# Issuing the transfers of the row maxima from ScalarE's queue, one unit behind their split, in an adaLN block with sliding-window attention

## The chip, the cores and the metric

The kernel runs on one core of one Trainium2 chip. The metric is the time on the device in microseconds (us): the median of three runs, 703.54 us before the change (703.54, 703.71 and 696.3). One further execution was profiled; it took 700.14 us, of which 698.3 us lie between its first and its last instruction.

## The reference

A transformer block on x of 2048 rows by 448 columns, in float32, with six modulation vectors from a condition c. What matters here is the attention: 16 heads of 28 columns, each row sees itself and the 255 rows before it.

```python
mod = (_silu(c) @ w_mod).reshape(c.shape[0], 6, 1, -1)
h = _layernorm(x, axis=-1) * (1 + ca) + sa
scores = jnp.einsum("bhqd,bhkd->bhqk", q, k) * (Dh ** -0.5)
mask = (idx[:, None] - idx[None, :] >= 0) & (idx[:, None] - idx[None, :] < W)
p = _softmax(jnp.where(mask[None, None], scores, -1e9), axis=-1)
x = x + ga * ((p @ v) @ wo)
h = _layernorm(x, axis=-1) * (1 + cb) + sb
x = x + gb * (mish(h @ w1 + b1) @ w2)
```

## The kernel before, in words

The 2048 rows are worked on in four groups of 512. A matrix product is made in three passes over a high and a low part of each operand, so most results are split once by ScalarE (high part) and once by VectorE (low part).

**Three stages.** Up to about 60 us weights are loaded, the first layer norm and the first products for q, k and v are made. From about 60 to 395 us runs the attention, with the products of the next group, the output product of the last one and the loads of the second half's weights filled in between. After that come the two products of the second half (lines 807 and 989 to 991), where TensorE is busy without a break.

**Slots, units and quartets.** In the attention a *slot* is one head of one group, 64 in all. Four slots make a *quartet*. q and k go to DRAM (`scr`) and come back by `L` (line 562) with the 28 columns of a head in three copies, as 84 partitions. There are eight tiles for q (four pairs, `Q2`) and eight for k, so slot i takes the tiles of slot i-8.

- `A(i, t)` (lines 571 to 582) makes the scores of 128 rows (PE, tile `sA`, two banks) and VectorE takes each row's maximum under the mask (`mx`).
- `M2(pr)` (line 584) serves a *pair* of slots, 32 pairs in all: PE transposes the eight columns of maxima (`mt`), VectorE splits them into a high and a low part (`mr`, lines 588 and 589), and two transfers write these as partitions 84 and 85 of the pair's q tile, where k holds -1. So the next product gives score minus maximum.
- `B(u)` (line 604) is one of 192 *units*: PE writes the mask and then q times k into one of two banks `sB` (lines 620 and 622), ScalarE takes the exponential (`P`, line 625). Twelve units make a quartet: unit u belongs to slot 4*(u//12) + u%4.
- `PV` and `EV` (lines 627 and 639) multiply four units' `P` with v five units later, and ScalarE copies a quartet's result out (`o`).

**What sets the order.** Each engine and each queue works in the order of the program; the loop over units (lines 925 to 971) writes it out by hand. With r = u mod 12, the maxima of the next quartet's four slots are worked on by `A` in units 1 to 10; `M2` stands in r = 7 for its first pair and in r = 11 for its second (line 943). The four slots of the quartet after are loaded in r = 8, 11, 2 and 4 (line 945). The first pair's tile is read from the next quartet's unit 0 on, the second pair's from its unit 2 on. So the second pair has three units between `M2` and its first reader.

All transfers go through SyncE's queue (`dma`, line 58, so their line in the profile is 59). An instruction at its head that waits keeps all behind it waiting. The two transfers of `M2` wait for the split; the next slots' loads stand right behind them, and wait only until PE has read the tiles that they overwrite. Transfers share eight semaphores: one is issued only when the transfer that had its semaphore before, mostly eight places back in the program, has landed.

Of the kernel before, what the change touches and what calls it, by code (L numbers as in the profile page):

```python
# [8 lines left out]
F32 = mybir.dt.float32  # L9
# [11 lines left out]
NQ, NK, NV = 8, 8, 10  # L21
# [30 lines left out]
def adaln_block(ctx: ExitStack, tc: tile.TileContext, x, wqkv, wo, w1, b1, w2, c, w_mod, out):  # L52
    nc = tc.nc
    PE, ACT, DVE, POOL = nc.tensor, nc.scalar, nc.vector, nc.gpsimd
# [3 lines left out]
    def dma(o, i):  # L58
        nc.sync.dma_start(o, i)  # L59
# [25 lines left out]
    def bank(tag, bufs, name):  # L85
        return PS[0].tile([128, 512], F32, name=name, tag=tag, bufs=bufs)
# [14 lines left out]
    for k in range(4):  # L101
        t = st0.tile([112, 2 * D], F32, name=f"wm01_{k}")
# [10 lines left out]
    for part in range(3):  # L113
        for ci in range(4):
            r0, r1 = ci * 128, min(ci * 128 + 128, D)
            for h in ((slice(0, 128),) if ci < 3 else (slice(0, 64), slice(64, 128))):
                t = wqs[ci][h]
# [172 lines left out]
    def drain(*gs):  # L290
        for g in gs:
            for _ in g:
                pipe.step()
# [16 lines left out]
    def flush():  # L310
        while later:
            later.pop(0)()
# [117 lines left out]
    Q2 = [att.tile([86, 2, GT], F32R, name=f"q2_{i}") for i in range(NQ // 2)]  # L430
    Q3 = [Q2[i // 2][:, i % 2] for i in range(NQ)]
    K3 = []
    for i in range(NK):
        t = att.tile([86, GT + W], F32R, name=f"k3_{i}")
# [121 lines left out]


    NS = NG * H
    mx, Pt, pvb, et, O4 = {}, {}, {}, {}, {}
    junk = att.tile([128, 384], BF16, name="junk")  # L560

    def L(i):
        g, h = divmod(i, H)
        q, k = Q3[i % NQ], K3[i % NK]
        f0, f1 = h * DH, D + h * DH
        q0, k0 = g * GT, max(g * GT - W, 0)
        l0 = k0 - (g * GT - W)
        dma(q[0:84, :].bitcast(F32), scr[f0:f0 + DH, :, q0:q0 + GT].rearrange("d a n -> (d a) n"))
        dma(k[0:84, l0:].bitcast(F32), scr[f1:f1 + DH, :, k0:q0 + GT].rearrange("d a n -> (d a) n"))

    def A(i, t):
        g, h = divmod(i, H)
        q, k = Q3[i % NQ], K3[i % NK]
        if i % 2 == 0 and t == 0:
            mx[i // 2] = att.tile([128, 2, 4], F32, name=f"mx{i}", tag="mx", bufs=2)
        c0 = max(256 - 128 * t, 0) if g == 0 else 0
        p = bank("sA", 2, f"sA{i}_{t}")
        PE.matmul(p[:, c0:384], q[0:84, t * 128:(t + 1) * 128], k[0:84, t * 128 + c0:t * 128 + 384],  # L578
                  start=True, stop=True)
        DVE.tensor_tensor_reduce(out=junk[:, c0:384], in0=p[:, c0:384], in1=mask[:, c0:384], scale=1.0,  # L580
                                 scalar=-3.0e38, op0=ALU.add, op1=ALU.max,
                                 accum_out=mx[i // 2][:, i % 2, t:t + 1])

    def M2(pr):
        p = bank("tr", 1, f"mt{pr}")
        PE.transpose(p[0:8, 0:128], mx[pr].rearrange("p a t -> p (a t)"), ident)
        r = att.tile([8, 2, 128], F32R, name=f"mr{pr}", tag="mr", bufs=2)
        DVE.tensor_copy(r[:, 0], p[0:8, 0:128])
        DVE.tensor_tensor(r[:, 1], p[0:8, 0:128], r[:, 0].bitcast(F32), op=ALU.subtract)
        for i in range(2):  # L590
            dma(Q2[pr % (NQ // 2)][84 + i:85 + i].bitcast(F32).rearrange("o a (t n) -> o (a t) n", t=4),
                r[:, i].bitcast(F32))

    def units(g, b):
        return [x for x in BLOCKS[b] if g > 0 or x[0] >= 2]
# [8 lines left out]
    def B(u):  # L604
        i, b = unit(u)
        g, h = divmod(i, H)
        q, k = Q3[i % NQ], K3[i % NK]
        bl = units(g, b)
        c0 = bl[0][3]
        p = bank("sB", 2, f"sB{u}")  # L610
        far = {c + 128 * (jj - t0) for jj, t0, t1, c in bl if t0 <= jj < t1}
        diag = {c + 128 * (jj - 2 - t0) for jj, t0, t1, c in bl if t0 <= jj - 2 < t1}
        masked = []
        for c in sorted(far | diag):
            if c in far:
                masked.append((256 if c + 128 in diag else 128, c, 0))
            elif c - 128 not in far:
                masked.append((128, c, 128))
        for i, (n, c, m) in enumerate(sorted(masked)):
            PE.matmul(p[:, c:c + n], identr, fdmask[:, m:m + n], start=(i == 0), stop=False, skip_group_check=True)  # L620
        for jj, t0, t1, c in by_width(bl)[::-1]:
            PE.matmul(p[:, c:c + 128 * (t1 - t0)], k[:, jj * 128:(jj + 1) * 128], q[:, t0 * 128:t1 * 128],  # L622
                      start=False, stop=True, skip_group_check=True)
        P = Pt[u] = att.tile([128, 512], F32, name=f"P{u}", tag="P", bufs=7)
        ACT.activation(P[:, c0:], p[:, c0:], AF.Exp, scale=SCALE)  # L625

    def PV(w):
        q, b = divmod(w, 3)
        g, h = divmod(4 * q, H)
        if b == 0:  # L630
            pvb[q] = bank("pv", 1, f"pv{q}")
        for n, (jj, t0, t1, c) in enumerate(by_width(units(g, b))):
            j = 4 * g - 2 + jj
            for a in range(4):
                PE.matmul(pvb[q][32 * a:32 * a + 32, t0 * 128:t1 * 128], V[j % NV][:, h + a, :],  # L635
                          Pt[4 * w + a][:, c:c + 128 * (t1 - t0)],
                          start=(b == 0 and n == 0), stop=False, skip_group_check=True)

    def EV(q):
        O4[q] = att.tile([128, GT], F32, name=f"o4_{q}", tag="o4")  # L640
        ACT.activation(O4[q], pvb[q], AF.Copy)
# [229 lines left out]
    def side_step(g, two):  # L871
        i = g == NG - 1
        if not (told.get(i) == "bank" and pipe.held() or told.get(i) == "dve" and two):
            told[i] = next(side[i], None)
# [7 lines left out]
    def step(g):  # L882
        return next(fillers[g], 99.0) or RATE[g]

    def need(keys, g):
        if all((g, m) in done for m in keys):
            return
        flush()
        while not all((g, m) in done for m in keys):
            pipe.step()  # L890
            try:
                next(fillers[max(g - 1, 0)])
            except StopIteration:
                next(fillers[g])
            flush()

    def load_slot(i):
        if i >= NS:
            return
        g, h = divmod(i, H)  # L900
        f0, f1 = h * DH, D + h * DH
        need({f0 // 128, (f0 + 27) // 128, f1 // 128, (f1 + 27) // 128}, g)
        L(i)
# [6 lines left out]
    for i in range(4):  # L910
        for t in range(4):
            A(i, t)
            if t % 2:
                pipe.step()
                next(fillers[0])
                flush()
            side_step(0, False)
        if i % 2:
            pipe.step()
            next(fillers[0])  # L920
            M2(i // 2)
        load_slot(4 + i)
    NU = 3 * NS
    credit = 0.0
    for u in range(NU + 7):
        s, k = divmod(u, 3)
        g = s // H
        if k == 0 and s % H == 0 and 0 < g < NG:
            drain(fillers[g - 1], *side[:g == NG - 1])
            flush()  # L930
        pipe.step()
        w, m = divmod(u - 5, 4)
        if m == 0 and 0 <= w < NU // 4:
            PV(w)
            if w % 3 == 2:
                EV(w // 3)
        if u < NU:
            B(u)
        q, r = divmod(u, 12)
        tiles = [divmod(n, 4) for n in range(16) if 1 + n * 10 // 16 == r and 4 * q + 4 < NS]  # L940
        for a, t in tiles[:1]:
            A(4 * q + 4 + a, t)
        if r in (7, 11) and 4 * q + 4 < NS:
            M2(2 * q + 2 + (r == 11))
        for a in range(4):
            if (u - (8, 11, 14, 16)[a]) % 12 == 0 and u >= (8, 11, 14, 16)[a]:
                load_slot(4 * ((u - (8, 11, 14, 16)[a]) // 12) + 8 + a)
        if r - 3 in (0, 1) and 0 <= (u - 12 - 3) // 12 < NS // 4:
            (E, E2)[r - 3](q - 1)
        if g < NG:  # L950
            v = u - 48 * g
            if v in (0, 2):
                chunk["v"] = 4 if v == 0 and g or 0 < g < NG - 1 else 2
            if v == 0:
                credit = 0.0
            credit += RATE[g] * (2 if v < FRONT[g] else 1)
            while credit > 0.0:
                credit -= step(g)
            if v > 1:
                side_step(g, len(tiles) > 1)  # L960
            if later and r in (1, 4, 5, 6, 8, 9):
                later.pop(0)()
        if u == NU:
            drain(fillers[NG - 1], side[1])
            while pipe.items:
                pipe.step()
            flush()
        if u - NU in TAIL:
            TAIL[u - NU]()
        for a, t in tiles[1:]:  # L970
            A(4 * q + 4 + a, t)
# [98 lines left out]
```

## Time and profile before

| | us |
|---|---|
| median of three runs (all) | 703.54 (703.54, 703.71, 696.3) |
| the profiled execution's own time | 700.14 |
| its span, first to last instruction | 698.3 |
| PE busy | 655.8 |
| VectorE busy | 346.6 |
| ScalarE busy | 280.8 |
| GpSimd busy | 98.2 |

The mean TensorE clock granted was 0.983 of full speed. In the profile "SPq" is SyncE's queue and "ACTq" an instruction of ScalarE's queue that only waits; `q<-mr` are the transfers of the maxima, `q<-scr` and `k<-scr` the loads of a slot, `scr<-st` the stores of q and k. In a timeline each row has its start, its duration, the engine and line, the tiles, and in brackets how long the engine was idle before it and what released it.

### The profile page before, as it was taken

To read this page: it belongs to the slowest core of one execution; us is meant where nothing else is said; L and a number is where in the kernel's file an instruction comes from. 1 tells how busy PE (TensorE), PEld (TensorE's weight loads), DVE (VectorE), ACT (ScalarE), POOL (GpSimd) and SP (SyncE) were. 2 spreads that over 40 slices of the span, in tenths; PEclk is the share of its full clock that TensorE was granted. 3 is DMA by queue.
4 is the path that set the end of the run, shared out by engine and by line. 5 is a ranking of instruction groups with operands and counts; after the bars stand their busy time and mean duration, and the time that the engine had idled before them with its cause. 6 is when DMAs were issued, how large, how long until landed. Compare 5 with 4: busy or idle time off the path is not lost.

```text
span 698.3 us, 10903 instructions
## 1 busy us (share of the span) xinstructions
PE 655.8 (94%) x3905; PEld 520.5 (75%) x3905; DVE 346.6 (50%) x934; ACT 280.8 (40%) x480; POOL 98.2 (14%) x150
## 2 busy tenths in 40 slices
PE   3876999989999999999998999999999999999996
PEld 3754666757777777777665788888888888888885
DVE  4826476745568766567778523434233313331112
ACT  3513444455444644353554853343233233332321
POOL 4632000032100300000001063421000000000002
PEclk9989899999999999999999999999999999999999
DMA  7665466648564746645474474103000110010001
GB/s 204 193 197 191 139 209 212 190 103 223 189 209 129 196 149 216 227 116 176 135 206 115 144 234 120 54 1 105 1 1 0 61 46 0 1 38 15 1 1 53
DMA packets 48114, 83.79 MB, mean 120 GB/s; under 512 B 6126, under 2 KB 26108, under 8 KB 48060
## 3 DMA queue, kind: packets, MB, share of 16 engines
q1 hardware_dynamic: 48060, 83.10, 39.1%
q8 instruction: 31, 0.51, 0.3%
q14 instruction: 23, 0.19, 0.1%
HBM read 53.45 MB, written 29.36 MB: 119 GB/s over the span
## 4 chain that ended last, share of the span: by engine, by line
PE 74%; issue 11%; DMA 6%; DVE 5%; SPq 2%; ACT 0%; POOL 0%; POOLq 0%; DVEq 0%; ACTq 0%
PE z L807 16%; PE qk L300 9%; PE sA L578 6%; PE pv L635 6%; PE sB L622 5%; PE wo L300 5%; PE acc L990 5%; PE acc L991 5%; PE acc L989 5%; PE sB L620 4%; PE qk_v L300 4%; DMA k<-scr 2%; SPq L59 2%; DVE junk L580 2%; DMA wm<-in_w_mod_dram 1%
## 5 line engine op out<-in xcount | busy, mean ns | idle before, releaser
L580 DVE CUSTOM_DVE_ANT_0 junk<-sA,mask 128x384 bf16<-128x384 f32 (+2 forms) x256 | 135.4, 529 | 106.6 <-PE sA L578 93.4
L625 ACT ACTIVATE P<-sB 128x512 f32<-128x512 f32 (+2 forms) x192 | 109.0, 572 | 141.1 <-PE sB L622 134.8
L815 DVE TENSOR_TENSOR al<-t,ah 128x512 fp32r<-128x512 f32 x56 | 38.8, 692 | 202.3 <-ACT ah L814 202.3
L813 ACT ACTIVATE t<-z,b1c 128x512 f32<-128x512 f32 x56 | 38.5, 687 | 189.4 <-PE z L807 178.5
L578 PE MATMUL sA<-k,q 84*128 84x384 f32 (+2 forms) x256 | 91.6, 368 | 14.8 <-DMA k<-scr 9.8
L622 PE MATMUL sB<-q,k 86*128 86x384 f32 (+1 forms) x352 | 90.7, 332 | 5.1 <-DMA q<-mr 5.1
L807 PE MATMUL z<-hhf,w 128*128 128x512 f32 x224 | 89.8, 401 | 0.0
L807 PE MATMUL z<-hlf,w 128*128 128x512 f32 x224 | 88.7, 396 | 0.0
L990 PE MATMUL acc<-w2l,ah 128*128 128x448 f32 x224 | 82.1, 367 | 0.0
L989 PE MATMUL acc<-w2h,ah 128*128 128x448 f32 x224 | 82.1, 367 | 0.0
L991 PE MATMUL acc<-w2h,al 128*128 128x448 f32 x224 | 82.1, 366 | 0.0
L578 PEld LDWEIGHTS sA<-k,q 84*128 84x128 f32 x256 | 49.2, 195 | 24.2 <-DVE mx L580 11.7
L807 PE MATMUL z<-hhf,w1l 128*128 128x512 f32 x168 | 66.4, 395 | 0.0
L620 PEld LDWEIGHTS <-identr 128*128 128x128 bf16 x320 | 21.9, 99 | 52.6 <-issue 50.0
L620 PE MATMUL sB<-fdmask,identr 128*128 128x128 bf16 (+1 forms) x320 | 60.3, 254 | 0.7 <-ACT P L625 0.7
L622 PEld LDWEIGHTS sB<-q,k 86*128 86x128 f32 x352 | 55.9, 195 | 6.2 <-DMA q<-mr 5.1
L635 PE MATMUL pv<-P,v 128*32 128x256 f32 (+2 forms) x704 | 50.5, 402 | 0.0
L807 PEld LDWEIGHTS z<-hlf,w 128*128 128x128 f32 x224 | 42.3, 189 | 9.8
L807 PEld LDWEIGHTS z<-hhf,w 128*128 128x128 f32 x224 | 42.3, 189 | 8.8 <-issue 0.6
L989 PEld LDWEIGHTS acc<-w2h,ah 128*128 128x128 f32 x224 | 42.1, 188 | 5.3
L990 PEld LDWEIGHTS acc<-w2l,ah 128*128 128x128 f32 x224 | 42.1, 188 | 5.2
L991 PEld LDWEIGHTS acc<-w2h,al 128*128 128x128 f32 x224 | 42.1, 188 | 3.6
(143 smaller groups left out, 991.0 us busy)
## 6 DMA issues: line engine op xcount, KB each, us to landing
scr<-st SPq DMA_DIRECT2D x24, 512.0 KB
k<-scr SPq DMA_DIRECT2D x48, 252.0 KB
q<-scr SPq DMA_DIRECT2D x64, 168.0 KB
scr<-st SPq DMA_DIRECT2D x32, 256.0 KB
x<-x1d SPq DMA_DIRECT2D x10, 448.0 KB
xin<-in_A_x_dram SPq DMA_DIRECT2D x8, 448.0 KB
xr<-in_A_x_dram SPq DMA_DIRECT2D x16, 224.0 KB
x1d<-xr SPq DMA_DIRECT2D x16, 224.0 KB
```

What stands on the lines that cost most here:

```text
L300: PE.matmul(p, b, a, start=(n == 0), stop=(n == 10))
L578: PE.matmul(p[:, c0:384], q[0:84, t * 128:(t + 1) * 128], k[0:84, t * 128 + c0:t * 128 + 384], start=True, stop=True)
L580: DVE.tensor_tensor_reduce(out=junk[:, c0:384], in0=p[:, c0:384], in1=mask[:, c0:384], scale=1.0, scalar=-3.0e38, op0=ALU.add, op1=ALU.max ...
L620: PE.matmul(p[:, c:c + n], identr, fdmask[:, m:m + n], start=(i == 0), stop=False, skip_group_check=True)
L622: PE.matmul(p[:, c:c + 128 * (t1 - t0)], k[:, jj * 128:(jj + 1) * 128], q[:, t0 * 128:t1 * 128], start=False, stop=True, skip_group_check= ...
L625: ACT.activation(P[:, c0:], p[:, c0:], AF.Exp, scale=SCALE)
L635: PE.matmul(pvb[q][32 * a:32 * a + 32, t0 * 128:t1 * 128], V[j % NV][:, h + a, :], Pt[4 * w + a][:, c:c + 128 * (t1 - t0)], start=(b == 0 ...
L807: PE.matmul(zb[n], ps[m][1], ps[m][0], start=(m == 0), stop=(m == 10))
L815: DVE.tensor_tensor(al[n], t, ah[n].bitcast(F32), op=ALU.subtract)
L989: PE.matmul(p, ah[n][:, ts], w2h[f], start=(f == 0), stop=False)
L990: PE.matmul(p, ah[n][:, ts], w2l[f], start=False, stop=False)
L991: PE.matmul(p, al[n][:, ts], w2h[f], start=False, stop=(f == NF - 1))
```

## The change

The two transfers leave `M2` and become `M3`, which issues them from ScalarE's queue. `M3` of a pair stands one unit behind its `M2`, at the end of that unit: in r = 8 for the first pair and in r = 0 of the next quartet for the second. Before the loop, `M3` follows its `M2` at once. Nothing else is altered; the tiles, the splits and all other transfers stay, and the number of transfers too.

```diff
-    mx, Pt, pvb, et, O4 = {}, {}, {}, {}, {}
+    mr, mx, Pt, pvb, et, O4 = {}, {}, {}, {}, {}, {}
...
         DVE.tensor_tensor(r[:, 1], p[0:8, 0:128], r[:, 0].bitcast(F32), op=ALU.subtract)
+        mr[pr] = r
+
+    def M3(pr):
         for i in range(2):
-            dma(Q2[pr % (NQ // 2)][84 + i:85 + i].bitcast(F32).rearrange("o a (t n) -> o (a t) n", t=4),
-                r[:, i].bitcast(F32))
+            ACT.dma_start(Q2[pr % (NQ // 2)][84 + i:85 + i].bitcast(F32).rearrange("o a (t n) -> o (a t) n", t=4),
+                          mr[pr][:, i].bitcast(F32))
...
             M2(i // 2)
+            M3(i // 2)
         load_slot(4 + i)
...
             M2(2 * q + 2 + (r == 11))
+        for i in range(2):
+            v = u - (7, 11)[i] - 1
+            if v % 12 == 0 and 0 <= v // 12 < NS // 4 - 1:
+                M3(2 * (v // 12 + 1) + i)
```

**SyncE's queue, around pairs 8 and 9** (the quartet that begins at about 138 us). `q<-mr` are the transfers in question, `q_2` and `k_5` the load of the slot that stands behind pair 9. Before:

```order
L59 DMA q_0_350<-mr_1440 1x8x128 x2
L59 DMA q_2_352<-scr 84x512
L59 DMA k_4_362<-scr 84x768
L59 DMA q_1_351<-mr_1513 1x8x128 x2
L59 DMA q_2_352<-scr 84x512
L59 DMA k_5_364<-scr 84x768
L59 DMA q_3_353<-scr 84x512
L59 DMA k_6_366<-scr 84x768
```

Now:

```order
L59 DMA wm_3_1331<-in_w_mod_dram 112x448
L59 DMA q_2_352<-scr 84x512
L59 DMA k_4_362<-scr 84x768
L59 DMA q_2_352<-scr 84x512
L59 DMA k_5_364<-scr 84x768
L59 DMA q_3_353<-scr 84x512
L59 DMA k_6_366<-scr 84x768
```

The loads follow one another; nothing that VectorE makes stands between them.

**ScalarE, at the same place.** `P<-sB` are the exponentials, the second row is the one of the new quartet's unit 0; `y` and `hh` evict a transposed chunk, `o` is the copy of `EV`. Before:

```order
L625 ACTIVATE P_1509<-sB_1504 128x512
L625 ACTIVATE P_1526<-sB_1521 128x512
L239 ACTIVATE y_1535<-tr_1530,cols 128x512
L236 ACTIVATE hh_1528<-tr_1530,cols 128x512
L641 ACTIVATE o_3_1546<-pv_1398 128x512
L625 ACTIVATE P_1553<-sB_1548 128x512
```

Now:

```order
L628 ACTIVATE P_1509<-sB_1504 128x512
L628 ACTIVATE P_1524<-sB_1519 128x512
L594 DMA q_1_351<-mr_1513 1x8x128 x2
L239 ACTIVATE y_1535<-tr_1530,cols 128x512
L236 ACTIVATE hh_1528<-tr_1530,cols 128x512
L644 ACTIVATE o_3_1546<-pv_1398 128x512
L628 ACTIVATE P_1553<-sB_1548 128x512
```

Two transfers stand behind the exponential of the quartet's unit 0 (`P_1524`); PE reads what they bring two units later.

**ScalarE, before the loop,** at about 62 us. Now:

```order
L236 ACTIVATE hh_596<-tr_598,cols 128x512
L594 DMA q_1_351<-mr_615 1x8x128 x2
L239 ACTIVATE y_612<-tr_607,cols 128x512
L236 ACTIVATE hh_596<-tr_607,cols 128x512
L628 ACTIVATE P_629<-sB_625 128x384
```

Without the second row this is the order of before; pair 1's transfers now stand ahead of the evictions and of the first exponential.

## The prediction

> **What bounds the kernel now.** I read the page first, then the waits, then the timelines of the places that the waits name.
>
> ```profile
> PE 655.8 (94%) x3905; PEld 520.5 (75%) x3905; DVE 346.6 (50%) x934; ACT 280.8 (40%) x480; POOL 98.2 (14%) x150
> PE 74%; issue 11%; DMA 6%; DVE 5%; SPq 2%; ACT 0%; POOL 0%; POOLq 0%; DVEq 0%; ACTq 0%
> ```
>
> PE sets the time: it is busy 94% of the span. Only its idle time can be won: 698.3 - 655.8 = 42.5 us. Much of that lies before 40 us and at the end, out of this change's reach. The chain spends 6% in transfers, ScalarE nothing. The waits name which transfers:
>
> ```profile
> PE sA L578 <- DMA k<-scr: 9.8, 4, 4.8
> PE sB L622 <- DMA q<-mr: 5.1, 3, 4.1
> SPq L59 <- DVE mr L589: 132.8, 29, 10.9
> L59 SPq DMA_DIRECT2D q<-mr x64: 627/640/1206, 56.4 to 381.8; - x64
> ```
>
> PE waits 9.8 us for keys and 5.1 us for the maxima. The third row is SyncE's queue: it stands 132.8 us waiting for VectorE's split, with the next loads behind it, and then needs 2 x 0.64 us for a pair's two transfers. Waiting of a queue costs nothing by itself; the question is where a load behind it came too late.
>
> **Part 1: the loads behind pair 9.** Rows of SyncE, then PE, then windows:
>
> ```profile
> 138.34 1.36 SPq L59 DMA_DIRECT2D q<-mr  x2
> 139.79 0.41 SPq L59 DMA_DIRECT2D q<-scr  x1
> 140.25 0.39 SPq L59 DMA_DIRECT2D k<-scr  x1
> ...
> 134.51 0.48 PE L622 MATMUL sB<-q,k 86*128 86x384 f32 x2
> ...
> 142.18 0.48 PE L622 MATMUL sB<-q,k 86*128 86x384 f32 x2
> 145.77 0.41 PE L578 MATMUL sA<-k,q 84*128 84x384 f32 x1 [3.10 <-DMA k<-scr]
> ...
> 140.25 5.38 DMA k<-scr
> ...
> 142.79:146.20 3.41, 0.43 (x3) 0.46 (x4) 0.38 (x2) 0.79 (x2) 1.15 (x1) 1.00 1.01 264
> 146.20:149.61 3.41, 3.41 (x25) 2.85 (x27) 1.40 (x6) 1.77 (x3) 0.00 (x0) 0.50 0.61 162
> ```
>
> This load waits for nothing but the queue: the tiles that it overwrites were last read by the unit whose product ran at 134.51 to 134.99. Without the two transfers ahead of it, q is issued at about 135.1 and k at 135.6 instead of 140.25, 4.7 us earlier. With the same 5.38 us to landing the keys are there at 141.0, and PE, which came to this product at 142.66, finds them. That removes 3.10 us. The windows show a second loss: after the idle stretch the granted clock (the column after the five engines) is 0.50 for 3.41 us. A half clock over 3.41 us of work costs 1.7 us. Part 1: 3.10 + 1.7 = 4.8 us.
>
> **Part 2: the same elsewhere.**
>
> ```profile
> 210.89 4.00 DMA k<-scr
> 215.03 0.41 PE L578 MATMUL sA<-k,q 84*128 84x384 f32 x1 [1.10 <-DMA k<-scr]
> ...
> 363.47 3.10 DMA k<-scr
> 366.70 0.41 PE L578 MATMUL sA<-k,q 84*128 84x384 f32 x1 [0.81 <-DMA k<-scr]
> ```
>
> Both loads stand behind a second pair's transfers in the same way and come 5 us or more earlier. Gain: 1.10 + 0.81 = 1.9 us. The fourth wait for keys, 4.8 us at 44 us, lies before the first pair, and stays.
>
> **Part 3: pair 1, before the loop.**
>
> ```profile
> 63.65 0.28 DVE L589 TENSOR_TENSOR mr<-mt,mr 8x128 fp32r<-8x128 f32 x1
> 65.97 1.42 SPq L59 DMA_DIRECT2D q<-mr  x2
> 66.75 2.61 DMA q<-mr
> ...
> 63.23 0.78 ACT L239 ACTIVATE y<-tr,cols 128x512 f32<-128x512 f32 x1 [0.36 <-PE tr L232]
> ...
> 64.56 0.49 ACT L625 ACTIVATE P<-sB 128x384 f32<-128x384 f32 x1
> ...
> 66.26 0.51 ACT L625 ACTIVATE P<-sB 128x384 f32<-128x384 f32 x1
> ...
> 69.49 0.66 PE L622 MATMUL sB<-q,k 86*128 86x384 f32 x1 [4.11 <-DMA q<-mr]
> 70.59 0.44 PE L620 MATMUL sB<-fdmask,identr 128*128 128x128 bf16 x2
> ...
> 67.69:71.10 3.41, 1.61 (x6) 1.29 (x6) 0.57 (x2) 0.49 (x1) 0.04 (x1) 0.50 0.74 249
> 71.10:74.52 3.42, 3.42 (x18) 2.05 (x17) 1.86 (x8) 2.21 (x4) 0.35 (x1) 0.50 0.28 107
> ```
>
> The split ends at 63.93, but SyncE comes to the transfers only at 65.97, and they land at 69.36. Now they start as soon as the split is done: the first at 63.6, the second ends its issue at about 65.0. With 2.0 us to landing (69.36 less 65.97 + 1.42) they are there at 67.0. But on ScalarE two evictions and the first exponential stand behind them: the eviction that began at 63.23 starts at 65.0, so the exponentials of 64.56 and 66.26 come about 1.8 and 1.9 us later, and PE's next two units need their banks: 66.9 and 68.7. The second of these began at 70.59. Gain 1.9 us. Of the two windows at half clock the first stays, I take it, since PE still idles from 64.65 to 66.9; the second needs not come: 1.7 us. Part 3: 3.6 us (1.9 if both windows stay).
>
> **Part 4: what the 64 transfers cost on ScalarE.** The trace of before has no transfer on ScalarE. Taken at SyncE's 0.64 to 0.69 us each, a pair occupies its queue for 1.36 us. For first pairs this is covered: their reader comes four units later, and the next exponential mostly starts later than the issue ends. Second pairs are the tight ones: `M3` stands behind the exponential of unit 0, and the transfers must land before unit 2. Two unknowns: whether the issue starts with that exponential or only at its end, and how long it takes to land. On the first, a row tells something:
>
> ```profile
> L320 ACTq EVENT_SEMAPHORE x6: 17/28/38, 87.8 to 99.6; - x6
> 87.73 0.49 ACT L625 ACTIVATE P<-sB 128x384 f32<-128x384 f32 x1 [1.03 <-PE sB L622]
> ...
> 381.03 1.35 SPq L59 DMA_DIRECT2D q<-mr  x2
> 381.75 1.76 DMA q<-mr
> ```
>
> The waiting instruction of the eviction behind this exponential ran at 87.8, while the exponential ran from 87.73 to 88.22. So ScalarE's queue goes on when an instruction has been handed over, and I let `M3` start with the exponential. Landing is 1.13 us after the issue at pair 31 (383.51 less 381.03 + 1.35) and 2.0 us in the busy stretch of pair 1. Of the fifteen second pairs the tightest and the last, each with unit 0's exponential and PE's first read:
>
> ```profile
> 323.90 0.60 ACT L625 ACTIVATE P<-sB 128x512 f32<-128x512 f32 x1 [2.76 <-PE sB L622]
> 325.66 0.48 PE L622 MATMUL sB<-q,k 86*128 86x384 f32 x2
> ...
> 381.18 0.60 ACT L625 ACTIVATE P<-sB 128x512 f32<-128x512 f32 x1 [0.82 <-PE sB L622]
> 383.65 0.47 PE L622 MATMUL sB<-q,k 86*128 86x384 f32 x2 [0.35 <-DMA q<-mr]
> ```
>
> 323.90 + 1.36 + 1.13 = 326.39, 0.7 us too late; at 381.18 it is 383.67, 0.4 us behind the 383.30 at which PE came. The same subtraction over all fifteen gives 2.2 us of lateness in sum at 1.13 us to landing and 10.6 us at 2.0; with the start at the exponential's end 6.5 and 17.3 us. I take the start with the exponential and 1.5 us to landing, since the loads now move just when the second pair does: 4.8 us, call it 5 (2 to 17). What stands behind `M3` on ScalarE (the evictions, `o`, the next exponential) starts up to 0.9 us later at nine of the fifteen places. I cost that at nothing: PE needs the next exponential's bank only two units on. Without that cover it is 9 x 0.9 = 8 us.
>
> The Trainium skill (Trace Analysis, Sequencer Loop) says that the sequencer pushes an engine's instruction into a queue and reads on; by that the price is the smaller pair of bounds, as I have it, and no run here shows it yet for a transfer.
>
> A transfer also waits for the earlier one on its semaphore. For the second transfers of pairs 9, 15 and 23 that is a load two or three places ahead, one of those that parts 1 and 2 bring forward. Pair 15's landed at 214.89; 5 us earlier it is there in time.
>
> **Sum.** 4.8 + 1.9 + 3.6 = 10.3 us won, 5 us given back: 5 us net. 700.1 - 5 = **695 us**. The profiled execution lies 3.4 us below the median of the runs and 3.8 us above the lowest, so I add nothing. About 1% is what a measurement here can tell from no change.
>
> **Rivals.** *Late at every second pair (slower).* The wait for keys is replaced by a wait for the maxima. If the issue starts only at the exponential's end and landing takes 2.0 us, the price is 17.3 us; what is held on ScalarE adds about 3. 20.3 - 10.3 = 10: **710 us**. It decides as soon as the lateness passes 10.3 us, about 2.0 us to landing with the early start, 1.5 with the late one. For it: the loads crowd into the units where `M3` stands. Against it: the ACTq row, and the 1.13 us.
>
> *Hidden anyway.* In 142.79 to 146.20 the DMA engines are busy all the time (1.01, 264 GB/s). If they and not the queue's order set the landing, the loads gain nothing from an early issue; parts 1 and 2 fall, 3.6 - 5 remain: **701 us**. Against it: the stretch before, in which the queue waited, has room (0.42, 96 GB/s):
>
> ```profile
> 139.38:142.79 3.41, 3.18 (x24) 2.26 (x20) 1.88 (x7) 3.41 (x7) 1.39 (x2) 1.00 0.42 96
> 374.89:378.30 3.41, 3.41 (x24) 1.81 (x24) 1.70 (x7) 0.99 (x2) 0.24 (x1) 0.50 0.26 66
> ```
>
>  The Trainium skill (DMA: Bandwidth & Descriptors, Issuing engines are not separate DMA queues) speaks for this rival: issuing from several engines saves only the time of issue. The rows put the gain elsewhere, in what waits behind a waiting instruction.
>
> *More is won.* All second pairs land in 1.13 us (2.2 us of cost), and the half clock window at 374.89 (the second row above), which follows small waits, does not come: 10.3 + 1.7 = 12; 12 - 2.2 = 9.8 us: **690 us**.
>
> **How the numbers follow.** Forecast 0.45, more won 0.15, hidden 0.28, late 0.12. The forecast's own range is 691 to 699. Against the runs' median 703.5 the forecast is 1.2% faster, against the profiled execution 0.7%; of its 0.45 I count 0.28 as faster by over 1% and 0.17 as within. Faster 0.28 + 0.15 = 0.43, same 0.17 + 0.28 = 0.45, slower 0.12. For 8 in 10 the range reaches from 688, a little below *more*, to 704, beyond *hidden* by the spread of the runs; most of *late* is left out.
>
> **What would show it.** In the changed profile: no row of SPq waiting for `mr`; PE's waits for keys down from 9.8 to about 5 us (the one at 44 us); at 63 to 75 us PE goes on about 2 us earlier; the clock stays at 1.00 near 146 us; PE's waits for the maxima come to about 5 us, spread over second pairs; transfers on ACTq start within 0.1 us of an exponential's start. The prediction is wrong if the waits for keys stay, if waits for the maxima pass 10 us, or if ScalarE's exponentials become PE's releaser.

## The result, and the profile after

The changed kernel takes 733.5 us at the median of four runs (724.8 to 737.2), the kernel before 703.6 in the same comparison: 1.042 times the time, 95% interval 1.036 to 1.048. It is 30 us slower; 695 us had been forecast, with 688 to 704 as the range.

The page of the profile after, its busy times and its chain, then the rows of the waits and of the transfers that answer to those of before:

```profile
PE 674.6 (92%) x3905; PEld 536.8 (73%) x3905; DVE 347.1 (47%) x934; ACT 281.1 (38%) x480; POOL 97.6 (13%) x150
...
PE 62%; issue 10%; DMA 7%; DVE 4%; ACT 1%; POOL 0%; SPq 0%; ACTq 0%; POOLq 0%; DVEq 0%
```

```profile
PE sB L625 <- DMA q<-mr: 25.0, 12, 4.0
PE sA L578 <- DMA k<-scr: 4.2, 1, 4.2
PE sB L625 <- DMA q<-scr: 3.0, 1, 3.0
```

The span is 732.0 us, 33.7 more than before. It divides without rest: PE's idle time grew from 42.5 to 57.4 us (14.9), and PE was busy 674.6 instead of 655.8 us (18.8) with the same 3905 instructions. The idle part is in the waits: the maxima 25.0 us instead of 5.1, the keys 4.2 instead of 9.8. The third row belongs to the maxima too: pair 21 lands at 299.20, 0.02 us before the load on which the profile books this wait. The busy part goes with the clock: all windows of the trace at half clock add up to 65.6 us, before to 25.1. That sum alone is no price: run 2 below has 41.9 us of such windows, and PE is busy only 658.3 us there.

Where it happens, at pair 9. The timeline of SyncE's and ScalarE's queues in the kernel after, and the chain of waits at the same place:

```profile
145.71 0.31 SPq L59 DMA_DIRECT2D q<-scr  x1
146.06 0.39 SPq L59 DMA_DIRECT2D k<-scr  x1
146.61 0.31 SPq L59 DMA_DIRECT2D q<-scr  x1
146.96 0.39 SPq L59 DMA_DIRECT2D k<-scr  x1
147.45 1.48 SPq L59 DMA_DIRECT2D wop<-in_A_wo_dram  x2
...
147.50 1.35 ACTq L594 DMA_DIRECT2D q<-mr  x2
```

```profile
148.23 4.89 DMA q<-mr
153.12 0.14 issue
153.25 0.76 PE sB L625 x2
```

```profile
149.61:153.02 3.41, 0.67 (x6) 0.35 (x4) 1.05 (x4) 3.11 (x6) 1.49 (x2) 1.00 0.83 225
153.02:156.43 3.41, 3.18 (x13) 2.83 (x14) 1.57 (x5) 1.19 (x2) 1.04 (x1) 0.50 0.00 0
156.43:159.85 3.42, 3.42 (x23) 2.54 (x25) 1.28 (x6) 1.93 (x3) 0.00 (x0) 0.50 0.02 5
```

In the kernel before, the pair's transfers came first, at 138.34, and the loads stood behind them. Now two loads and a piece of a weight are issued in the 3.2 us before the end of the pair's second issue. That end is at 148.86, and the pair lands at 153.12: 4.26 us, where pair 9 took 1.14 us before. PE then idles 2.97 us, and the windows show the rest of the bill: the two after the wait run at a clock of 0.50. The DMA share falls from 0.83 to 0.00 there: with the pair, all that was in flight has landed.

In what follows, **landing** is the time from the end of issue of a pair's second transfer to the completion that its semaphore shows.

### The profile page after: what moved, and what is told of

Its sections match the earlier page's. It is cut to its first block, busy times and chain, and to the rows that moved or that the text cites. A ratio compares the mean times of both kernels' runs of the same rounds, so it can differ in the third digit from the quotient of the medians.

```text
span 732.0 us, 10880 instructions
## 1 busy us (share of the span) xinstructions
PE 674.6 (92%) x3905; PEld 536.8 (73%) x3905; DVE 347.1 (47%) x934; ACT 281.1 (38%) x480; POOL 97.6 (13%) x150
## 4 chain that ended last, share of the span: by engine, by line
PE 62%; issue 10%; DMA 7%; DVE 4%; ACT 1%; POOL 0%; SPq 0%; ACTq 0%; POOLq 0%; DVEq 0%
PE z L810 15%; DMA q<-mr 6%; PE sA L578 5%; PE sB L625 5%; PE qk L300 5%; PE wo L300 5%; PE acc L998 5%; PE acc L999 5%; PE acc L997 5%; PE pv L638 4%; PE qk_v L300 3%; PE sB L623 3%; DVE junk L580 1%; PE et L649 1%; PE trf L232 1%
## 5 line engine op out<-in xcount | busy, mean ns | idle before, releaser
L625 PE MATMUL sB<-q,k 86*128 86x384 f32 (+1 forms) x352 | 96.3, 350 | 28.1 <-DMA q<-mr 25.0
L578 PE MATMUL sA<-k,q 84*128 84x384 f32 (+2 forms) x256 | 96.6, 389 | 6.2 <-DMA k<-scr 4.2
L625 PEld LDWEIGHTS sB<-q,k 86*128 86x128 f32 x352 | 60.1, 209 | 31.8 <-DMA q<-mr 14.7
L623 PE MATMUL sB<-fdmask,identr 128*128 128x128 bf16 (+1 forms) x320 | 62.7, 263 | 1.3 <-ACT P L628 1.3
L578 PEld LDWEIGHTS sA<-k,q 84*128 84x128 f32 x256 | 53.1, 211 | 13.5 <-DVE mx L580 5.6
```

## The experiments

Three theories stood at the start. **A:** the loads of the next slots are no longer held behind the split, so they are in flight when the maxima go out, and the maxima land late among them. **B:** what ScalarE's queue issues lands late as such. **C:** the unit of delay in `M3` costs the time. The table has all runs; waits are PE's, landing is the median over the sixteen first and the sixteen second pairs, half clock is the sum over the span. The kernel before took 702.5 to 703.6 us beside them.

| run | maxima issued from | us | ratio, 95% interval | landing, first / second | wait for maxima | half clock |
|---|---|---|---|---|---|---|
| before | SyncE, at once | 703.6 | 1 | 1.14 / 1.14 | 5.1 | 25.1 |
| after | ScalarE, a unit behind | 733.5 | 1.036 to 1.048 | 2.80 / 3.11 | 25.0 | 65.6 |
| 1 | ScalarE, at once | 717.2 | 1.015 to 1.028 | 2.61 / 3.39 | 17.6 | 41.4 |
| 2 | SyncE, a unit behind | 698.9 | 0.992 to 0.998 | 1.14 / 1.14 | 8.9 | 41.9 |
| 3 | after, loads held to the split | 729.3 | 1.029 to 1.045 | 2.62 / 3.09 | 25.9 | 56.9 |
| 4 | after, small loads | 710.3 | 1.007 to 1.015 | 2.03 / 2.14 | 13.9 | 30.3 |
| 5 | 1, loads held to the landing | 727.1 | 1.030 to 1.039 | 1.15 / 1.61 | 0.5 | 54.7 |
| 6 | SyncE, loads put ahead | 720.3 | 1.019 to 1.032 | 1.73 / 1.65 | 21.9 | 43.4 |
| 7 | 2, pairs 0 and 1 ScalarE | 697.0 | 0.990 to 0.996 | 1.14 / 1.93 | 7.6 | 22.2 |
| 8 | first pairs ScalarE, second SyncE | 695.8 | 0.986 to 0.993 | 2.88 / 1.14 | 3.5 | 28.6 |
| 9 | first SyncE, second ScalarE | 737.5 | 1.042 to 1.055 | 1.14 / 3.77 | 28.5 | 67.8 |
| 10 | 8, a load behind the second pair | 703.9 | 0.999 to 1.005 | 2.82 / 1.14 | 3.4 | 31.3 |
| 11 | 8, second pairs at once | 696.6 | 0.984 to 0.994 | 2.98 / 1.14 | 1.5 | 35.6 |

**Runs 1 and 2: one part of the change alone.**

```diff
-        for i in range(2):
-            v = u - (7, 11)[i] - 1
-            if v % 12 == 0 and 0 <= v // 12 < NS // 4 - 1:
-                M3(2 * (v // 12 + 1) + i)
+            M3(2 * q + 2 + (r == 11))
```

> The changed kernel, but the transfers of the maxima are issued from ScalarE's queue at once, in the unit of their split. Theory A (the loads of the next slots, no longer held back by the split, are in flight when the maxima go out, and the maxima land late among them): landing after the issue stays at 2 to 4.5 us, the time at 715 to 735 us, little won by the earlier issue because ScalarE's queue now waits for the split. Theory B (ScalarE's queue itself is slow to land): the same landing, 715 to 735 us. Theory C (the unit of delay is what costs): about 700 us.

```diff
-            ACT.dma_start(Q2[pr % (NQ // 2)][84 + i:85 + i]...
+            nc.sync.dma_start(Q2[pr % (NQ // 2)][84 + i:85 + i]...
```

> The changed kernel, but the transfers of the maxima go through SyncE's queue, still one unit behind their split. Theory A: first pairs, whose transfers stand ahead of the next load, land in 1.1 to 1.6 us; second pairs, which now stand behind a load, land 2.5 to 5 us after their issue; 715 to 735 us. Theory B: all land in 1.1 to 1.6 us, 698 to 706 us. Theory C: all land in 1.1 to 1.6 us but second pairs are issued a unit late, about 705 to 715 us.

Without the delay the loss is half as large, without ScalarE's queue it is gone: 698.9 us, faster than before. C falls: the same delay in SyncE's queue costs nothing. On run 2 it was B's forecast that held (698 to 706 us) and A's that missed (715 to 735): A had taken each second pair to stand right behind a load, but the loads ahead of them had begun their issue 1.6 us or more earlier, and only 7 of the 32 pairs had anything ahead that was in flight for another 1.3 us. So far it is the queue, or what the queue changes. The waits and the queue of run 2:

```profile
PE sB L625 <- DMA q<-mr: 8.9, 8, 4.6
PE sA L578 <- DMA k<-scr: 3.0, 1, 3.0
```

```profile
118.15 1.23 SPq L59 DMA_DIRECT2D q<-scr  x1
119.43 0.95 SPq L59 DMA_DIRECT2D k<-scr  x1
120.48 1.37 SPq L594 DMA_DIRECT2D q<-mr  x2
...
139.21 1.36 SPq L594 DMA_DIRECT2D q<-mr  x2
140.66 0.41 SPq L59 DMA_DIRECT2D q<-scr  x1
```

One pair shows what counts. Pair 7 (120.48) has a load right ahead of it, whose second transfer was issued 1.05 us before, and lands after 2.37 us, from SyncE; pair 9 (139.21) has the next load behind it, the last one ahead has landed before its issue ends, and it lands after 1.14 us.

**Runs 3 and 4: the loads held, the loads made small.**

```diff
+    hold = dram.tile([64, 8, 128], F32, name="hold")
...
+        for i in range(2):
+            dma(hold[2 * pr + i], r[:, i].bitcast(F32))
         mr[pr] = r
```

> The changed kernel, and in SyncE's queue, where the transfers of the maxima stood, two transfers of the same size that copy the split to a scratch in DRAM, so that the loads behind them are held until the split is done, as before the change. Theory A: the maxima land 1.1 to 1.8 us after their issue from ScalarE's queue, and the time is 698 to 710 us although nothing of the change is undone. Theory B: landing stays at 2 to 4.5 us and the time at 725 to 740 us. Theory C: landing is short, but the late issue keeps the time at 715 us or more.

```diff
-        dma(q[0:84, :].bitcast(F32), scr[f0:f0 + DH, :, q0:q0 + GT]...
-        dma(k[0:84, l0:].bitcast(F32), scr[f1:f1 + DH, :, k0:q0 + GT]...
+        n = DH if i < NQ else 9
+        m = DH if i < NK or 2 * NK <= i < 3 * NK else 9
+        dma(q[0:3 * n, :].bitcast(F32), scr[f0:f0 + n, :, q0:q0 + GT]...
+        dma(k[0:3 * m, l0:].bitcast(F32), scr[f1:f1 + m, :, k0:q0 + GT]...
```

> The changed kernel with the loads of q (from slot 8 on) and k (slots 8 to 15 and from 24 on) cut to 9 of 28 columns in their three copies, 27 of 84 partitions, so about a third of the bytes in the same number of transfers; the other partitions keep an older slot's values, so the scores are left wrong. Theory A: the maxima land in 1.1 to 2 us, PE's waits for them fall under 6 us in sum and the half-clock windows after them go; under 700 us, as PE's waits for keys go too. Theory B: landing stays at 2 to 4.5 us, 725 us or more.

Run 3 looks like a defeat of A, 729 us where A had 698 to 710. Its queue tells why it was a bad test:

```profile
142.60 0.62 SPq L59 DMA_DIRECT2D hold<-mr  x2
143.31 0.31 SPq L59 DMA_DIRECT2D q<-scr  x1
143.67 0.48 SPq L59 DMA_DIRECT2D k<-scr  x1
...
142.69 1.35 ACTq L597 DMA_DIRECT2D q<-mr  x2
```

Holding the loads to the split lets go at the moment at which ScalarE goes too. Of the next load q is out before the pair's second issue ends at 144.04, k as it ends, and the pair lands at 146.85. Run 4 leaves 7.8 us of the loss of 30: with less data ahead a pair lands after some 2.1 us. That is between the two theories (under 700 us for A, 725 or more for B) and decides neither.

So I set the landings of all pairs against what was issued ahead of them, from either queue and still in flight. In the kernel after, 29 of 32 pairs have something ahead that is in flight for another 1.3 us or more, and they land on average 0.11 us after the last of it, with a spread of 0.30 us (one standard deviation); the correlation of the two times over all pairs is 0.95. The other three land in 1.15 to 1.17 us: pairs 30 and 31 have nothing ahead, pair 20 one load that lands 0.1 us after it. This is A in a sharper form: **a pair completes with the transfers that were issued just ahead of it, whichever queue they came from; the queue itself doesn't matter.** In the kernel before, the same waiting that released the maxima released the loads, but 1.5 us behind them (139.79 after 138.34 at pair 9).

The trace also tells whether the data come late or only the completion, since it has the packets of each queue: q1 is SyncE's queue, q10 ScalarE's, with packets, MB and the share of the time of the 16 DMA engines. At pair 9, first from 148.90 to 150.60, then from 150.60 to 152.10:

```profile
q1 hardware_dynamic: 203, 0.44, 102.1%
...
q1 hardware_dynamic: 232, 0.39, 98.2%
q10 hardware_dynamic: 32, 0.01, 3.1%
```

For 1.7 us after the pair's issue the DMA engines work for SyncE's queue alone; then all 32 packets of the pair run. The first starts at 150.70, 2.57 us after the issue of its transfer ended; at pair 31, with nothing ahead, that takes 0.65 us. So the data are late. Over the 29 pairs the last packet of data ends 2.51 us after the issue at the median and the completion follows 0.75 us later; at pair 31 these are 0.74 and 0.41 us.

**Runs 5 and 6: order against queue.** Run 5 keeps ScalarE's queue and puts all loads behind the landing (a small transfer of SyncE reads the two rows of maxima); run 6 keeps SyncE's queue and puts the loads of one slot ahead.

```diff
+            M3(2 * q + 2 + (r == 11))
...
+        dma(hold[pr], Q2[pr % (NQ // 2)][84:86].bitcast(F32))
```

> The run with both transfers on ScalarE directly behind their split (717 us), plus one small transfer of SyncE per pair that reads the two rows of maxima back to DRAM, so that SyncE stands until the pair has landed and the next loads go out only then. Theory A, in its sharper form (the queue does not matter; a pair lands behind the transfers that were issued just ahead of it, from whichever queue): nothing is issued ahead any more, so landing after the end of issue is 1.1 to 1.4 us at most pairs, as in the kernel before, PE's waits for the maxima are 4 to 9 us, and the time is 700 to 712 us; a few us over the kernel before, since the loads now wait for the landing and not for the split. Theory B (a transfer from ScalarE's queue lands late as such): landing stays at 2.3 to 5 us, and with the loads later too the time is 717 to 732 us.

```diff
+        if pr > 1:
+            dma(hold[pr], r[:, 0].bitcast(F32))
...
-            ACT.dma_start(...
+            nc.sync.dma_start(...
...
+        for a in range(4):
+            if (u - (8, 12, 14, 16)[a]) % 12 == 0 and u >= (8, 12, 14, 16)[a]:
+                load_slot(4 * ((u - (8, 12, 14, 16)[a]) // 12) + 8 + a)
         for i in range(2):
             v = u - (7, 11)[i] - 1
```

> All on SyncE's queue, one unit behind the split, as in the run of 699 us, but with the order turned: in the loop a small transfer to DRAM holds the queue until the split, then come the loads of one slot, and only behind them the pair's two transfers. ScalarE issues nothing. Theory A: in the loop the pairs land 2 to 4 us after the end of their issue, as from ScalarE; with the issue itself up to 1.6 us later PE waits 20 to 40 us for the maxima, and the time is 718 to 745 us. Theory B: landing stays at 1.14 us, only the later issue costs, about 11 us of waits: 704 to 714 us.

Pair 9 in run 5, queues, then chain, then waits:

```profile
148.52 0.22 SPq L59 DMA_DIRECT2D hold<-q  x1
148.79 0.31 SPq L59 DMA_DIRECT2D q<-scr  x1
149.15 0.38 SPq L59 DMA_DIRECT2D k<-scr  x1
...
146.01 1.35 ACTq L595 DMA_DIRECT2D q<-mr  x2
```

```profile
146.73 1.77 DMA q<-mr
...
149.15 4.40 DMA k<-scr
```

```profile
PE sA L579 <- DMA k<-scr: 27.7, 12, 4.1
...
PE sB L627 <- DMA q<-mr: 0.5, 2, 0.3
```

From ScalarE the median landing is 1.15 us again and PE waits 0.5 us for the maxima. B falls. The time that A expected was wrong all the same, 727 for 700 to 712: the loads now come too late, and PE waits 27.7 us for keys. I had priced the hold at a few us and not followed it to the keys' reader.

Run 6 at pair 9, queue and chain:

```profile
142.41 0.31 SPq L59 DMA_DIRECT2D q<-scr  x1
142.78 0.38 SPq L59 DMA_DIRECT2D k<-scr  x1
143.21 1.36 SPq L597 DMA_DIRECT2D q<-mr  x2
```

```profile
143.94 3.44 DMA q<-mr
147.38 0.14 issue
```

With SyncE's queue alone, the same 2.81 us to landing at this pair (1.14 before), 21.9 us of waits for the maxima, and 720 us: inside A's range, outside B's. Its landings, 1.1 to 3.9 us, stay below A's 2 to 4 at most pairs, because only one load stands ahead and the pair's own issue gives it 1.4 us to be done; part of the waits is the later issue.

**Runs 7, 8 and 9: which pairs.** The edit is the issuing engine alone.

```diff
+            (ACT if pr < 2 else nc.sync).dma_start(...                    # run 7
+            (ACT if pr < 2 or pr % 2 == 0 else nc.sync).dma_start(...     # run 8
+            (ACT if pr < 2 or pr % 2 else nc.sync).dma_start(...          # run 9
```

> Pairs 0 and 1, before the loop, from ScalarE; all in the loop from SyncE, one unit behind. The run with all on SyncE waits 4.56 us for pair 1, the changed kernel 1.39 us, because there the issue needn't stand behind SyncE's other work. Both theories: the wait for pair 1 falls by 2 to 3 us, the rest stays: 694 to 698 us. If the stretch before the loop is bound by something else, 698 to 700 us.

> First pairs of a quartet (and pair 1) from ScalarE, second pairs from SyncE, all one unit behind. If the loss of the changed kernel is the late landing of second pairs alone (first pairs land 3 to 5 us before they are needed), first pairs may land 2 to 5 us after their issue and cost nothing: 693 to 702 us, PE's waits for the maxima 4 to 10 us. If instead 32 transfers on ScalarE cost by what they hold there (the next exponential, evictions), half of the loss stays: 712 to 720 us, with ScalarE's exponentials as PE's releaser.

> The mirror of the run of 696 us: first pairs from SyncE, second pairs (and pairs 0 and 1) from ScalarE, all one unit behind. If the second pairs carry the loss, because SyncE's loads are issued just ahead of them and they have no slack, they land 2 to 5 us after their issue as in the changed kernel, PE waits 15 to 25 us for the maxima, several windows at half clock follow, and the time is 714 to 732 us. If it takes both kinds of pair on ScalarE to lose, 696 to 704 us.

Run 7 came as expected, 697.0 us: the wait for pair 1 fell from 4.56 to 1.67 us. Against run 2 the gain isn't clear of the noise. The waits of run 8, then those of run 9:

```profile
PE sA L578 <- DMA k<-scr: 4.3, 1, 4.3
PE sB L625 <- DMA q<-mr: 3.5, 7, 1.2
```

```profile
PE sB L625 <- DMA q<-mr: 28.5, 12, 4.6
...
PE sB L625 <- DMA q<-scr: 6.5, 2, 3.3
```

In run 8 first pairs from ScalarE land as late as in the changed kernel, 2.88 us at the median and up to 4.56, and cost next to nothing, 0.15 us at pair 28: they are needed 3 to 5 us after an early landing. The mirror loses all that the change lost, and a little more (its range reached 732, it took 737.5); the two waits on `q<-scr` are those of pairs 7 and 21, which land 0.05 and 0.03 us before that load. So the loss is the second pairs'; what 34 issues hold on ScalarE costs nothing that shows. Run 8 beats both kernels: 1.1% faster than before, interval 0.7 to 1.4%.

**Runs 10 and 11: around the best.**

```diff
-            if (u - (8, 11, 14, 16)[a]) % 12 == 0 and u >= (8, 11, 14, 16)[a]:
+            if (u - (8, 12, 14, 16)[a]) % 12 == 0 and u >= (8, 12, 14, 16)[a]:
```

> The run of 696 us with one edit: the second load of a quartet stands one unit later in the program, behind the second pair's transfers. Second pairs that still landed at 2.1 to 2.6 us there (pairs 17 and 21) land at 1.14. If the order decides, PE's waits for the maxima fall from 3.5 to 2 to 3 us; the load is issued up to one unit later, so the waits for keys (4.3 us) may grow by 1 to 4 us: 693 to 700 us. The price of holding a load shows there: if keys come late at many quartets, 700 to 710 us.

```diff
-            v = u - (7, 11)[i] - 1
+            v = u - (8, 11)[i]
```

> The run of 696 us with one edit: second pairs go out in the unit of their split, as in the kernel before, and SyncE stands there with the next load behind it; first pairs stay on ScalarE. If it was the standing of SyncE at second pairs that cost the kernel before its waits for keys (those after pairs 9, 15 and 29), they come back: 4 to 9 us of waits for keys instead of 4.3, and 697 to 703 us. If the unit of delay is worth nothing, 694 to 697 us.

Run 10, one load later, gives the gain back in waits for keys, of 13.7 us instead of 4.3. Pair 17 does land at 1.14 us there, pair 21 still at 2.16; the waits for the maxima stay at 3.4 us:

```profile
PE sA L578 <- DMA k<-scr: 13.7, 9, 2.8
```

Run 11 takes the time of run 8 within their spread: for second pairs from SyncE the unit of delay is worth nothing in sum. But the waits for keys did come back. Its rows of waits, and the one behind pair 9:

```profile
PE sA L578 <- DMA k<-scr: 5.0, 4, 2.2
PE sA L578 <- POOL k L435: 3.4, 1, 3.4
...
145.62 0.41 PE L578 MATMUL sA<-k,q 84*128 84x384 f32 x1 [2.19 <-DMA k<-scr]
```

The wait at 44 us is the second row here. Of the first, 2.19, 1.56 and 0.99 us stand behind pairs 9, 15 and 29, where the kernel before waited 3.10, 1.10 and 0.81. So the standing of second pairs in SyncE's queue costs these waits, whether first pairs stand there or not. The time doesn't show it: the waits for the maxima are 2.0 us less than in run 8, and the 2.7 us that are left lie within the spread of the runs.

## Why the prediction was wrong

**What failed is part 4, "1.5 us to landing".** Second pairs took 3.11 us at the median, up to 4.73; the cost of 5 us became 25.0 us of waits for the maxima, of which only 1.4 us are pair 1's and 1.4 us a first pair's (pair 6). The bounds, 1.13 and 2.0 us, were read at two pairs of the kernel before, where only 4 of 32 pairs have anything ahead that is in flight for another 1.3 us. The prediction said the right thing beside the wrong number, "since the loads now move just when the second pair does". And the trace of before held the price. SyncE's queue at pair 28:

```profile
349.83 1.17 SPq L59 DMA_DIRECT2D w1p<-in_B_w_dram  x2
351.10 1.04 SPq L59 DMA_DIRECT2D x<-x1d  x2
352.66 0.34 SPq L59 DMA_DIRECT2D x1d<-xr  x1
354.67 1.46 SPq L59 DMA_DIRECT2D q<-mr  x2
```

Five transfers within 5 us ahead, the last of which lands 3.21 us after the end of the pair's issue at 356.13; the pair's own completion comes at 359.94, 3.81 us after that end. It is a first pair, so PE didn't wait, and no view of waits lists it. Landing had to be read where transfers stand ahead, not where PE waits.

**Also part 4: the wait was priced, its clock was not.** In parts 1 and 3 a half-clock window went into the sum as a gain; the new waits of about 3 us got none. They brought 40.5 us more at half clock, and PE's busy time grew by 18.8 us: more than the idle time.

**Parts 1 and 2 were right as far as they went.** The wait for keys behind pair 9 and both smaller ones are gone; the 4.2 us that stay are the wait at 44 us. Run 11, where second pairs stand in SyncE's queue again, has these waits back. The window at 146.20 keeps a clock of 1.00. But 7 us further on, at 153.02, pair 9's own lateness brings two windows at half clock. A quiet queue was what made the keys late and the maxima early; the prediction took the first and thought the second free.

**Part 3 was right in its wait and wrong in what it left.** PE comes to pair 1's product at 66.95 instead of 69.49. Three windows at half clock follow (67.69 to 77.93) where there were two, and by the end of unit 12 only 0.5 us is left (83.7 against 84.2).

**Right in part 4:** `M3` starts with the exponential (0.05 to 0.10 us behind its start at 25 of the 30 pairs in the loop), and what it holds on ScalarE costs little: PE's waits for an exponential are 1.3 us in sum instead of 0.7. At a first pair both queues wait for TensorE at the same point (the product that runs from 141.44 to 141.92 is the exponential's input and the last to read the tile that the load overwrites):

```profile
141.95 0.32 SPq L59 DMA_DIRECT2D q<-scr  x1
142.32 0.39 SPq L59 DMA_DIRECT2D k<-scr  x1
...
142.02 0.60 ACT L628 ACTIVATE P<-sB 128x512 f32<-128x512 f32 x1 [0.52 <-PE sB L625]
142.10 1.40 ACTq L594 DMA_DIRECT2D q<-mr  x2
```

At twelve of the fourteen first pairs from pair 2 to pair 28 the load starts 0.07 to 0.15 us ahead of the maxima; before, it started some 1.5 us behind them. Taking the wait out of SyncE's queue turned the order round.

**The rivals.** *Late at every second pair* is what happened, with a chance of 0.12 and a price of 710 us. Its point of decision, 2.0 us to landing, was right; its own landing, 2.0 us, was no bound. For *hidden anyway* the prediction cited the Trainium skill (DMA: Bandwidth & Descriptors, Issuing engines are not separate DMA queues). The Trainium skill (DMA: Bandwidth & Descriptors, Queues, rings and completion order) has a sentence that bears on the cause: the semaphore's increment lands only after every earlier write of that DMA engine, across its queues. The landings agree with it, 0.11 us behind the last transfer ahead; but most of the delay is there before the increment, in the data. The same section of the Trainium skill says that an engine takes turns between its queues packet by packet; by that alone one would expect a small transfer from a second queue to be served early among the loads, and at pair 9 it was not, for 2.57 us. What holds its packets back in that time, no run here tells.

## What to carry to other kernels

A wait at the head of a queue also sets an order: before taking it away, list what it keeps behind the urgent transfer, and who will be issued ahead once it is gone. Read a small transfer's landing time from the places where others were issued just ahead of it; quiet places give a floor, not a price. And move the transfers that have slack, not those that have none: here the first pairs on the second queue won 1.1%, the second pairs lost 4.8% (with pairs 0 and 1 on it in both runs).

## What the runs showed of the hardware

A pair's transfers of 4 KB each complete 1.14 us (SyncE's queue) or 1.15 us (ScalarE's) after their issue when nothing is ahead, and up to 6 us after it when loads from the other queue are (run 1, pair 7: 5.97 us); the packets of their data are late with them. A wait of some 3 us inside the attention costs about twice its length, by an estimate from the windows: of seven between 2.5 and 4.0 us in the changed kernel, six came with 6.83 us at half clock, about 3.4 us of work lost, and one with 3.41. In the kernel before, the wait of 3.10 us at 145.77 had a single window of 3.41 us.
